# Attention of batches three to eight in quarters of TensorE's array, before a Strassen feed-forward

## The chip, the cores and the metric

The kernel runs on one core of a Trainium2 chip. The metric is the device time of one execution in microseconds, the median of several runs. The profile shows one execution: TensorE (PE, with its weight loads PEld), VectorE (DVE), ScalarE (ACT), GpSimd (POOL), SyncE (SP, which issues the DMAs) and the DMA engines.

## What is computed

Eight batches of eight heads, 576 positions, head width 64, all in float32 at both ends. Heads 0 to 3 look back over a plain window of 32 positions, heads 4 to 7 over 32 positions with a step of 4. The result goes through a feed-forward layer of width 2048.

```python
scores = scale * np.matmul(q, k.transpose(0, 1, 3, 2))
rel = pos[:, None] - pos[None, :]
mask_plain = (rel >= 0) & (rel < window)
mask_dil = (rel >= 0) & (rel < window * dilation) & (rel % dilation == 0)
...
attn = attn / (np.sum(attn, axis=-1, keepdims=True) + 1e-09)
return np.matmul(attn, v).astype(np.float32)
...
h = x @ w_in
g = np.maximum(0.01 * h, h)
return (g @ w_out).astype(np.float32)
```

## The kernel before

All matmuls are in float16. The tokens of two batches (1152) are three chunks of 384. For each chunk the first layer (`up`, L1057, and `up_pair`, L1091; the last three chunks by Strassen's seven products in `ups7`, L1191) writes `gt` through a Prelu on ScalarE, and the second layer goes by tiles of 128 tokens, the first four plainly (`down`, L1271), all others in groups of four with seven products for eight (`group`, L1361).

Attention feeds `xt`, the input of the first layer. The program treats the heads of a batch in four pairs (`vi`, called visits, in the order 2, 3, 0, 1; 2 and 3 are dilated), each in two units (`unit`, L815 on). A pair lies on 128 partitions, 64 for each head. A stationary block of keys holds 64 keys of both heads, column by column in turn, with zeros in the half that belongs to the other head, so that one 128 x 128 block gives the scores of both. A unit has three groups of matmuls on TensorE, each between other work: the scores (L899, five matmuls of up to 96 columns), the sums of the exponentials (L924, against a constant block) and the values (L918, five matmuls). Between them ScalarE takes the exponential (L907), VectorE multiplies it with the mask (L911) and, for plain pairs, adds what overlaps (L932); after them ScalarE takes the logarithm of the sums and the exponential of its negative (L943, L945) and VectorE multiplies the values with it into `xt` (L956). Scores and values take the three PSUM banks `sps`, `ops0` and `ops1` in turn.

For the first two batches (`EARLY`) queries and keys are loaded in long rows and turned by TensorE (`turn_in`, L743), and the mask comes as a matmul of a bias. For batches three to eight they are loaded in rows of 32 numbers, cast by GpSimd (L505), turned by VectorE in blocks of 32 (L708, L713, L720), and spread into the zero-padded blocks by copies on ScalarE, GpSimd and VectorE (L516, L517, L714). The values are cast twice for each pair, once for each head, into columns in turn (L505).

The order is planned by the program itself: each piece of work is a task with an estimated duration and the pieces that it needs, a list scheduler runs over them several times, and the tables `NUDGE` (shifts of priority by task number) and `HAND` (a fixed engine for a task) change its choice. `WHEN` gives the time at which a batch's attention is due. The result is a fixed order on each engine's queue; each engine then works strictly in that order.

Of the kernel before, what the change touches and what calls it, by code (L numbers as in the profile page):

```python
# [14 lines left out]
WIN = 32  # L15
# [3 lines left out]
WHEN = (3.92, 2.82, 39.64, 80.18, 115.4, 117.81, 161.72, 152.03)  # L19
PASSES = 8  # L20
SEVEN = (9, 10, 11)
SECOND = 'st01t'
ADDED = (2, 9)
LAPS = ("DVE", "POOL")
# [91 lines left out]
    "DVE", 1623: "POOL", 1629: "POOL", 1633: "ACT", 1728: "DVE", 1740: "DVE"}  # L116


HELD = 4


def _constants():
# [246 lines left out]
def kernel(  # L369
# [19 lines left out]
    NJ = DFF // 128  # L389
    SCALE = float(1.0 / np.sqrt(D))  # L390
    HS = S * D
    EARLY = 2
    VISITS = (2, 3, 0, 1)

    const_d = nc.inline_tensor(_constants(), name="consts").ap()
# [1090 lines left out]
    for b in range(EARLY):  # L1486
        take_slots(b)
# [180 lines left out]
```

## Time and profile before

| | |
|---|---|
| time, three runs | 294.31 to 294.81 us, median 294.36 us |
| span of the profiled execution (no other time is given for it) | 292.5 us |
| granted TensorE clock | 1.00 |
| VectorE, ScalarE, GpSimd busy | 78%, 75%, 41% of the span |
| DMA queue q1, share of the DMA engines' time | 65.0% |
| first and last scores of batches three to eight | 64.0 us, 231.8 us |

The page gives busy time by engine, the span in 40 slices, the chain of work that ended last, and the costliest groups of instructions with their mean duration. A duration of a matmul reaches from its start until its last result is written; the next matmul starts long before that. Where the distance from one to the next is needed, it is read from the starts in the timeline.

### The profile page before, as it was taken

The page shows a single profiled execution, that of the slowest core. Times are in us where ns is not written, and L with a number is a line of the kernel's source. Part 1 is how long each engine was busy: PE and PEld are TensorE (multiplying, and loading weights), DVE is VectorE, ACT ScalarE, POOL GpSimd, SP SyncE. Part 2 cuts the span into 40 slices and gives each one's busy share as a digit, 9 for nine tenths or more (in the row PEclk, how much of TensorE's full clock was granted, in tenths as well). Part 3 has the DMA queues.
Part 4 walks back from the last instruction along what each step waited for, and adds up shares of the span by engine and source line. Part 5 has one row for each costly group of instructions (what it writes and reads, how often), then busy time and mean ns, then how long its engine had stood idle before and what let it go on. Part 6 is the DMA issues. An engine that isn't in the chain of part 4 may idle for free.

```text
span 292.5 us, 7626 instructions
## 1 busy us (share of the span) xinstructions
PE 285.2 (97%) x2924; PEld 226.4 (77%) x2924; DVE 226.8 (78%) x437; ACT 218.9 (75%) x483; POOL 121.2 (41%) x173
## 2 busy tenths in 40 slices
PE   6899999999999999999999999999999999999995
PEld 2567776776787788677777877887688999999985
DVE  7877588674799789858839889897878889678672
ACT  3997987589869966878888987888767966755522
POOL 5420452458537746964873774653425000000000
PEclk9999999999999999999999999999999999999999
DMA  7999999799898959999799798751101210121133
GB/s 244 267 389 396 395 377 224 150 168 218 142 188 185 179 144 174 191 168 208 197 170 160 180 205 151 195 134 59 36 2 36 75 38 0 38 74 36 38 109 110
DMA packets 156068, 47.15 MB, mean 161 GB/s; under 512 B 136832, under 2 KB 153344, under 8 KB 156032
## 3 DMA queue, kind: packets, MB, share of 16 engines
q1 hardware_dynamic: 155344, 46.04, 65.0%
q10 hardware_dynamic: 688, 0.63, 0.6%
q8 instruction: 23, 0.38, 0.5%
q14 instruction: 13, 0.11, 0.1%
HBM read 37.22 MB, written 9.44 MB: 160 GB/s over the span
## 4 chain that ended last, share of the span: by engine, by line
PE 93%; ACT 2%; DVE 2%; DMA 1%; issue 1%; ACTq 0%; DVEq 0%
PE hps L1057 27%; PE fps L1361 23%; PE tp L1361 9%; PE hps L1191 5%; PE fps L1271 4%; PE hps L1091 4%; PE ops L1191 3%; PE ops L918 3%; PE ops L899 2%; PE sps L899 2%; PE ops L924 2%; PE sps L1191 1%; DMA con<-consts 1%; PE sps L924 1%; PE ops L1361 1%; PE sps L918 1%
## 5 line engine op out<-in xcount | busy, mean ns | idle before, releaser
L1057 PE MATMUL hps<-xt,w_in 128*128 128x384 f16 x488 | 94.7, 325 | 0.0
L1361 PEld LDWEIGHTS <-gt 128*128 128x128 f16 x768 | 73.0, 98 | 9.8 <-DVE gt L1347 0.2
L1073 ACT ACTIVATE gt<-hps 128x384 f16<-128x384 f32 x122 | 59.1, 487 | 13.7 <-PE hps L1057 12.7
L1057 PEld LDWEIGHTS <-w_in 128*128 128x128 f16 x512 | 44.9, 98 | 21.3 <-issue 0.3
L505 POOL CAST slots<-vst 128x576 f16<-128x576 f32 x55 | 46.0, 861 | 22.7 <-DMA vst<-in_v_dram 5.6
L505 POOL CAST nat<-stg 128x576 f16<-128x576 f32 (+1 forms) x52 | 34.6, 687 | 48.6 <-DVE gt L1347 15.1
L1361 PE MATMUL fps<-w_out,gt 128*128 128x256 f16 x368 | 46.7, 272 | 0.0
L911 DVE TENSOR_TENSOR ee<-ee,con 128x384 f16<-128x384 f16 (+1 forms) x48 | 20.6, 430 | 15.3 <-ACT ee L907 14.9
L945 ACT ACTIVATE rc<-rc 128x288 f32<-128x288 f32 (+1 forms) x64 | 27.2, 436 | 1.1
L956 DVE TENSOR_TENSOR xt<-ops,rc 128x288 f16<-128x288 f32 (+2 forms) x44 | 19.3, 445 | 9.7 <-ACT rc L945 4.9
L516 ACT COPY slots<-turned 64x512 f16<-64x512 f16 (+1 forms) x30 | 23.8, 799 | 0.8 <-DVE turned L708 0.5
L1214 ACT ACTIVATE gt<-vst 128x384 f16<-128x384 f32 (+1 forms) x24 | 16.0, 684 | 8.0 <-DVE vst L1210 8.0
L899 PEld LDWEIGHTS <-slots 128*128 128x128 f16 x308 | 18.1, 98 | 4.7 <-DVE slots L517 0.4
L517 POOL COPY slots<-turned 64x576 f16<-64x576 f16 (+2 forms) x25 | 16.7, 675 | 11.2 <-ACT slots L516 3.5
L907 ACT ACTIVATE ee<-ops 128x416 f16<-128x416 f32 (+2 forms) x35 | 16.7, 487 | 3.6 <-PE ops L899 3.0
L918 PEld LDWEIGHTS <-slots 128*128 128x128 f16 x308 | 17.1, 97 | 2.8 <-ACT slots L504 0.6
L924 PEld LDWEIGHTS <-con 128*128 128x128 f16 x168 | 14.0, 97 | 5.9 <-issue 0.8
L708 DVE STREAM_TRANSPOSE turned<-nat 128x576 f16<-128x576 f16 x24 | 18.0, 759 | 0.1
L1390 ACT COPY stg<-fps 128x512 f32<-128x512 f32 (+1 forms) x20 | 10.4, 519 | 9.4 <-PE fps L1361 9.1
L907 ACT ACTIVATE ee<-sps 128x416 f16<-128x416 f32 (+2 forms) x29 | 14.4, 495 | 3.8 <-PE sps L899 2.7
L1347 DVE TENSOR_TENSOR gt<-gt 128x1024 f16<-128x1024 f16 x21 | 16.6, 789 | 0.3 <-PE fps L1361 0.2
L1191 PEld LDWEIGHTS <-w_in 128*128 128x128 f16 x192 | 16.2, 98 | 0.2
(158 smaller groups left out, 559.8 us busy)
## 6 DMA issues: line engine op xcount, KB each, us to landing
out_dram<-osb SPq DMA_DIRECT2D x32, 256.0 KB, 2.6
stg<-in_k_dram SPq DMA_DIRECT2D x48, 144.0 KB, 3.6
stg<-in_q_dram SPq DMA_DIRECT2D x48, 144.0 KB, 3.4
vst<-in_v_dram SPq DMA_DIRECT2D x16, 288.0 KB, 4.3
vst<-in_v_dram SPq DMA_DIRECT2D x32, 128.0 KB, 3.2
gt<-in_moe_w_in_dram SPq DMA_DIRECT2D x6, 512.0 KB, 6.8
stg<-in_q_dram SPq DMA_DIRECT2D x3, 512.0 KB, 6.9
stg<-in_k_dram SPq DMA_DIRECT2D x3, 512.0 KB, 9.1
```

Source lines behind the costliest of these rows:

```text
L505: return ENG[e].tensor_copy(out=dst, in_=src)
L516: return nc.scalar.copy(out=dst, in_=src)
L899: nc.tensor.matmul(p_bank[:, c:c + w], slot(tn, KB + 128 * s, 0, 128, [1, 128]), slot(tn, qx, 0, 128, *qd), start=first or not by_pe, stop ...
L907: lambda e: nc.scalar.activation(out=et[:, 0:n], in_=p_bank[:, 0:n], func=AF.Exp, scale=SCALE), prio)
L911: lambda e: nc.vector.tensor_tensor(out=et[:, 0:n], in0=et[:, 0:n], in1=con[:, table:table + n], op=ALU.mult), prio,
L918: nc.tensor.matmul(at(dst, 0, 128, o, *od), lhs(s), et[:, c:c + w], start=i == 0, stop=i == len(steps) - 1, skip_group_check=True)
L924: nc.tensor.matmul(at(p_bank, 0, 128, o, *od), block_ones, at(et, 0, 128, c, *cd), start=i == 0, stop=i == len(rows) - 1, skip_group_check ...
L945: lambda e: nc.scalar.activation(out=rt, in_=rt, func=AF.Exp, scale=-1.0), prio)
L1057: nc.tensor.matmul(ht[:, 0:n], at(w_in, 0, 128, vi * DFF + j // 2 * 256 + j % 2, [2, 128]), at(xt[m % 2], 0, 128, vi * 1152 + x0 + x, [1, n]),
L1073: lambda e: nc.scalar.activation(out=gt[c % NG][:, j * n_c + x:j * n_c + x + n], in_=ht[:, 0:n], func=AF.Prelu, alpha=0.01),
L1191: nc.tensor.matmul(bk[:, n * i:n * i + n], w(v, 2 * z + i), x(v), start=first and i == 0 and v == 0, stop=i == 1 and v == 1, skip_group_ch ...
L1361: nc.tensor.matmul(bk[:, x:x + HN], tl[:, off + j * step:off + j * step + 128], rhs(j), start=first and x == 0 and j == 0, stop=j == HJ - ...
```

## The change

Batches three to eight no longer go through `unit`. Their attention goes through `burst`: one task on TensorE that holds the sums and values of one pair and the scores of a later one. Each matmul is 64 x 64: it names a quarter of the array by `tile_position`, takes its rows from 64 partitions and writes 64 partitions. Four such matmuls stand together, one for each quarter, and the two row halves write to different PSUM banks. No block is padded with zeros.

- Heads of a pair are neighbours (0 and 1, 2 and 3, ...), no longer one apart. So the rows of `w_in` for a pair are 128 rows on end, and one DMA loads them at once.
- Batch three (`PACKED = 3`) loads in long rows and is turned by TensorE, as the first two are. From batch four on, queries and keys lie as two pairs side by side, and the scores of two visits must be there before the values of either.
- The sums and values of a pair come one burst after its scores in batch three and two bursts after in the others.
- One exponential, one mask multiplication, one logarithm and one reciprocal for a pair, over 576 to 896 columns in two PSUM banks, in place of two each over 288 to 416; the additions for overlaps are gone. The multiplication into `xt` has two parts.
- A burst takes four banks: `ops0`, `ops1`, `sps` and one that the group of the second layer does not use just then (`lent`).
- Queries and keys of plain pairs are turned by VectorE straight to their place; those of dilated pairs need one more copy each, on GpSimd or ScalarE (L910). The copies into padded blocks and the constant for them are gone. The values are cast once for a pair.
- Values are loaded in 14 DMAs a batch in place of 8.
- All PSUM is one tile `psum`, cut into the same eight banks. `NUDGE` and `HAND` have new numbers throughout, since the tasks are others; `WHEN` has only its first two entries, and bursts are placed every `PACE` groups of the first layer from `PLACE` on.

```diff
-WHEN = (3.92, 2.82, 39.64, 80.18, 115.4, 117.81, 161.72, 152.03)
+WHEN = (3.92, 2.82)
...
+PLACE = 20.0
+PACE = 4.7
+SWITCH = 0.3
...
-    EARLY = 2
+    EARLY, PACKED = 2, 3
...
+        if b >= EARLY:
+            lv = []
+            for i in range(2):
+                p = 64 * i
+                if g:
+                    lv += [load(queue, at(vs, p, p + 64, 128 * n, [320, 4], [1, 128]),
+                                dram(v, base + (256 * n + 2 * i) * D, [4 * D, 64], [HS, 4], [1, 128]),
+                                256, 512, v_old, prio + 0.01 * n) for n in range(2)]
...
-            src = dram(moe_w_in, heads_of(vi)[0] * D * DFF + x, [DFF, 64], [2 * D * DFF, 2], [1, 1024])
+            src = dram(moe_w_in, 128 * vi * DFF + x, [DFF, 128], [1, 1024])
...
+    def burst(now, then, prio, lent):
+
+        seats = [ops[0], ops[1], lent, sps]
+        room, mine = {}, {}
+        for bk in seats:
+            room[key(bk)], mine[key(bk)] = grab(bk)
...
+        def product(bk, x, od, lhs, rhs, p, q, first, last):
+            p0, p1, q0, q1 = quarter(p, q)
+            jobs.append(lambda: nc.tensor.matmul(
+                at(bk, q0, q1, x, *od), lhs(p0, p1, q), rhs(p0, p1), start=first, stop=last,
+                skip_group_check=True, tile_position=(p0, q0)))
...
+            for n, two in enumerate(list(zip(sums_of(vi, 0), sums_of(vi, 1)))
+                                    + list(zip(values_of(vi, 0), values_of(vi, 1)))):
...
+            for _, c, w, keys, asks in places(b2, v2):
+                for p in range(2):
+                    for q in range(2):
+                        def lhs(p0, p1, _, k=keys[q]):
+                            return slot(t2, KB + k[1], p0, p1, k[0])
...
+            t_l = add("ACT", 0.07 + S / 1200.0, [t_b] + r_old,
+                      lambda e: nc.scalar.activation(out=at(rt, 0, 128, 0, [288, 2], [1, 288]),
+                                                     in_=both(1, 224, None, [1, 288]), func=AF.Ln), prio)
+            t_r = add("ACT", 0.105 + S / 1200.0, [t_l],
+                      lambda e: nc.scalar.activation(out=rt, in_=rt, func=AF.Exp, scale=-1.0), prio)
...
+    pairs, due = [], []
+    for b, vi in [(b, vi) for b in range(EARLY, B) for vi in VISITS] + [(B, None)] * 2:
+        pairs.append((due.pop(0) if due else None, (b, vi) if b < B else None))
+        if b < PACKED:
+            due.append((b, vi))
+        elif b < B and vi % 2:
+            due += [(b, vi - 1), (b, vi)]
```

The first place is TensorE in the middle of the program. Before, the values of one dilated unit stand between two groups of the first layer (`hps` is their bank, `ee` the exponentials, `slots` the values of a pair). Rows that only repeat are left out.

```order
L1057 MATMUL hps_103<-xt_87,w_in 128x384
L918 LDWEIGHTS slots
L918 MATMUL ops_101<-ee_81,slots 128x96
L918 MATMUL ops_101<-ee_81,slots 128x80
L918 MATMUL ops_101<-ee_81,slots 128x2x16
L1057 LDWEIGHTS w_in
L1057 MATMUL hps_102<-xt_87,w_in 128x384
```

Now, again between groups of the first layer (L1378 is its line now), a burst stands in one piece: sums against the constant `con`, values from `slots`, and the scores of a later pair.

```order
L1378 MATMUL psum<-xt_78,w_in 128x384
L1256 LDWEIGHTS con
L1256 MATMUL psum<-ee,con 64x96
L1256 MATMUL psum<-ee,con 64x64
L1256 MATMUL psum<-ee,con 64x32
L1256 LDWEIGHTS slots
L1256 MATMUL psum<-ee,slots 64x64
L1256 MATMUL psum<-slots 64x96
```

What stood in three to six places of the queue stands in one, 64 to 68 matmuls long. There are 26 such pieces: the first and the sixth have scores alone, the last two none.

The second place is ScalarE. Before, the two units of a plain pair go through it one after the other, between the Prelu of the first layer (L1073).

```order
L907 ACTIVATE ee_81<-sps_104 128x416
L1073 ACTIVATE gt_88<-hps_103 128x384
L907 ACTIVATE ee_82<-ops_101 128x416
L1390 COPY osb_91<-fps_105 128x512
L943 ACTIVATE rc_83<-sps_104 128x288
L945 ACTIVATE rc_83<-rc_83 128x288
L943 ACTIVATE rc_84<-ops_101 128x288
L945 ACTIVATE rc_84<-rc_84 128x288
```

Now, at the fourth and the fifth burst: L1346 is the exponential of the scores, L1318 and L1321 the logarithm and the exponential of its negative, L1394 the Prelu.

```order
L1346 ACTIVATE ee<-psum 128x896
L1318 ACTIVATE rc<-psum 128x576
L1394 ACTIVATE gt_82<-psum 128x384
L1321 ACTIVATE rc<-rc 128x576
L1394 ACTIVATE gt_82<-psum 128x384 x3
L1346 ACTIVATE ee<-psum 128x2x384
L1394 ACTIVATE gt_82<-psum 128x384
L1318 ACTIVATE rc<-psum 128x576
```

Six instructions of a pair became three, each about twice as wide, and they stand closer together behind their burst.

More of the change, by code (lines that the diff above doesn't have):

```diff
@@ L119 @@
 HELD = 4
+TURN_AT = ('st01t', 'ssss0')
+DOWN_ON = (0, 1)
 def _constants():
@@ L696 @@
     x_done, x_used = {}, {b: [] for b in range(-2, B)}
+    seat_of = {'f': fps[0], 'g': fps[1], 's': sps, '0': ops[0], '1': ops[1], 't': tpb}
     def turn(b, vi, prio):
@@ L1176, in ups7 @@
             h = z // 2
-            ring5 = five if c > 9 else [hps[0], hps[1], ops[1]]
-            X, Y, Z = (ring5[(five_at[0] + i) % len(ring5)] for i in range(3))
+            X, Y, Z = (five[(five_at[0] + i) % len(five)] for i in range(3))
             five_at[0] += 3
@@ L1485 @@
     t_con = [None]
-    for b in range(EARLY):
+    for b in range(2):
         take_slots(b)
@@ L1516, in attend @@
         else:
-            banks = dict.fromkeys(VISITS, [sps, ops[0]] if b == 7 and 9 in SEVEN else three)
+            banks = dict.fromkeys(VISITS, three)
         for n, vi in enumerate(VISITS):
@@ L1525, with place, bursts @@
     wide_banks = {2: fps[0], 3: fps[1], 4: tp32, 5: sps, 6: ops[0], 7: ops[1]}
+    pairs, due = [], []
+    for b, vi in [(b, vi) for b in range(EARLY, B) for vi in VISITS] + [(B, None)] * 2:
+        pairs.append((due.pop(0) if due else None, (b, vi) if b < B else None))
+        if b < PACKED:
+            due.append((b, vi))
+        elif b < B and vi % 2:
+            due += [(b, vi - 1), (b, vi)]
+    assert not due
+    flow, lent, n_up, weights = [0], [tp32], [0.0], {}
+    def place(k):
+        return PLACE + PACE * k
+    def bursts(upto, prio):
+        while flow[0] < len(pairs) and place(flow[0]) <= upto:
+            now, then = pairs[flow[0]]
+            if then is not None:
+                b, vi = then
+                if vi == VISITS[0]:
+                    fetch(b, prio, 6.5)
+                if b < PACKED:
+                    if vi == VISITS[0]:
+                        turn_rest(b, prio)
+                    turn(b, vi, prio)
+                elif vi == VISITS[0]:
+                    for v in VISITS:
+                        turn(b, v, prio)
+                then = take(b, vi)
+            flow[0] += 1
+            burst(now, then, prio, lent[0])
     def ups(c, x, n, batches, js=(0, NJ)):
@@ L1592 @@
     order.sort(key=lambda t: (t.start, t.n))
-    slow = next(t for t in order if t.eng == "POOL" and t.kind == "cast" and t in ups_at[0].deps)
+    slow = next((t for t in order if t.eng == "POOL" and t.kind == "cast" and t in ups_at[0].deps), None)
     kept = [t for t in order if t.eng == "ACT" and t.start < ups_at[1].start]
-    if slow.start < kept[-1].start:
+    if slow is not None and slow.start < kept[-1].start:
         slow.eng, slow.start = "ACT", kept[-1].start + 1e-4
```

474 lines of the change are left out of this document (294 added, 180 removed), and 306 rows, old and new, of the table NUDGE.

## Prediction

> **What bounds the kernel now.** I read the page first (busy shares and the chain that ended last), then the busy time of each engine in two stretches, then the waits of TensorE, and last the timeline of TensorE around the attention of the later batches.
>
> ```profile
> PE 285.2 (97%) x2924; PEld 226.4 (77%) x2924; DVE 226.8 (78%) x437; ACT 218.9 (75%) x483; POOL 121.2 (41%) x173
> PE 93%; ACT 2%; DVE 2%; DMA 1%; issue 1%; ACTq 0%; DVEq 0%
> 24.00:236.00 212.00, 211.65 (x2166) 164.07 (x2163) 166.99 (x321) 172.13 (x386) 112.15 (x155) 1.00 0.76 172
> 236.00:292.50 56.50, 53.55 (x551) 49.85 (x549) 40.72 (x81) 29.15 (x58) 0.00 (x0) 1.00 0.17 57
> PE tp L743 <- ACT nat L504: 0.7, 1, 0.7
> PE ops L924 <- ACT ee L907: 0.3, 1, 0.3
> ```
>
> The first two lines are from the page, the next two are the stretches (span, then busy time of PE, PEld, DVE, ACT and POOL), the last two are waits. TensorE is busy for 211.65 of the 212 us from 24 to 236, at a granted clock of 1.00, and it is 93% of the chain. Its waits on another engine are single ones of 0.7 and 0.3 us. So the time of this kernel is the sum of TensorE's stream, and a change is worth what it takes from that stream, less the waits that it brings. A busy matmul overlaps the next one, so durations can't be added: what counts is the distance from the start of one group to the start of the next.
>
> ```profile
> 81.64 0.35 PE L899 MATMUL sps<-slots 128*128 128x96 f16 x5
> 81.83 1.03 PE L1361 MATMUL fps<-w_out,gt 128*128 128x256 f16 x8
> ...
> 101.69 0.34 PE L918 MATMUL ops<-ee,slots 128*128 128x96 f16 x5
> 101.88 0.33 PE L924 MATMUL ops<-ee,con 128*128 128x192 f16 x3
> 102.05 0.33 PE L918 MATMUL sps<-ee,slots 128*128 128x96 f16 x5
> ...
> 106.31 0.30 PE L924 MATMUL sps<-ee,con 128*128 128x32 f16 x3
> 106.45 0.35 PE L918 MATMUL ops<-ee,slots 128*128 128x96 f16 x5
> 106.64 1.03 PE L1361 MATMUL fps<-w_out,gt 128*128 128x256 f16 x8
> 107.52 0.29 PE L924 MATMUL ops<-ee,con 128*128 128x160 f16 x2
> 107.64 0.60 PE L1361 MATMUL fps<-w_out,gt 128*128 128x256 f16 x4
> ```
>
> Here the first column is the start. One group of scores (L899, five matmuls) holds TensorE for 81.83 - 81.64 = 0.19 us. A group of values (L918) holds it for 0.19 us (101.69 to 101.88, 106.45 to 106.64). A group of sums (L924) takes 0.17 us where it is dilated (three matmuls, 101.88 to 102.05), and 0.14 and 0.12 us for the two halves of a plain pair (106.31 to 106.45, 107.52 to 107.64).
>
> **What is removed.** Batches 3 to 8 have 24 head pairs of two units each.
>
> ```profile
> L899 PEld LDWEIGHTS <-slots x240: 95/98/99, 64.0 to 231.8; 128*128 128x128 f16 x120
> L918 PEld LDWEIGHTS <-slots x240: 95/98/99, 67.8 to 235.3; 128*128 128x128 f16 x120
> L924 PEld LDWEIGHTS <-con x132: 95/98/99, 66.3 to 234.8; 128*128 128x128 f16 x132
> ```
>
> These are the instructions of those batches alone, from 64 us on: 240 / 5 = 48 groups each of scores and values, and 132 matmuls of sums. Removed are 48 x 0.19 = 9.1 us of scores, 48 x 0.19 = 9.1 us of values, and 24 x 0.17 + 12 x 0.14 + 12 x 0.12 = 7.2 us of sums: 25.4 us together.
>
> **What is added on TensorE.** The scores of before stream 416 columns for a plain half in 0.19 us, so 0.46 ns a column. In the new bursts the 1584 matmuls of L1256 come in 396 sets of four, one for each quarter of the array. One quarter streams 448 + 416 + 416 = 1280 columns for a plain pair and 3 x 384 = 1152 for a dilated one, so 12 x 1280 + 12 x 1152 = 29184 in all. If the four quarters run side by side, that is 29184 x 0.46 ns = 13.4 us. Batch 3 is now turned by TensorE: 32 transposes and 4 for its last rows.
>
> ```profile
> 8.94 0.39 PE L791 MATMUL fps<-con,rest 128*128 128x128 f16 x4
> 9.16 0.39 PE L743 MATMUL fps<-con,nat 128*128 128x128 f16 x4
> ```
>
> Four transposes hold TensorE for 0.22 us, so 36 cost 2.0 us. The stream alone is 13.4 + 2.0 - 25.4 = **-10.0 us**.
>
> **Changing over.** TensorE enters and leaves the quarters 26 times. No matmul in quarters is in this trace, so I bound the price of one change-over.
>
> ```profile
> L899 PE MATMUL sps<-slots x110: 179/206/213, 64.2 to 231.8; 128*128 128x96 f16 x61, 128*128 128x80 f16 x22, 128*128 128x32 f16 x17, 128*128 128x64 f16 x10
> ```
>
> A matmul of 96 columns lasts 206 ns and streams for 96 x 0.46 = 44, so its last 0.16 us is a tail that the next matmul normally overlaps. Below: nothing, the quarters overlap with the full array just so. Above: the tail is waited out on entering and on leaving, 52 x 0.16 = 8.3 us. No row is nearer to one end than to the other, so I take one tail for each burst, 26 x 0.16 = 4.2 us, and keep both ends.
>
> The Trainium skill (TensorEngine Tiling (Array Packing), Key Properties) says that a change of the tiling mode, not of the tile alone, drains TensorE. It speaks for the upper end, no run so far shows it, and by it the sum would be 4.1 us higher than mine.
>
> **New waits.** Before, a unit's Exp, Ln and reciprocal are separate and short, and there are three PSUM banks in turn. A burst takes four banks at once (three of them always the same), and the next burst can't start before ScalarE and VectorE have emptied them.
>
> ```profile
> L907 ACT ACTIVATE ee<-sps 128x384 f16<-128x384 f32 x11 | 5.4, 489 | 0.7 <-issue 0.5 <-PE sps L899 0.2
> L907 ACT ACTIVATE ee<-sps 128x320 f16<-128x320 f32 x4 | 1.8, 438 | 0.3 <-PE sps L899 0.3
> L943 ACT ACTIVATE rc<-ops 128x288 f32<-128x288 f32 x27 | 10.8, 409 | 3.2 <-PE ops L924 3.1
> L945 ACT ACTIVATE rc<-rc 128x288 f32<-128x288 f32 x52 | 22.4, 442 | 0.9
> L956 DVE TENSOR_TENSOR xt<-ops,rc 128x288 f16<-128x288 f32 x38 | 16.8, 449 | 7.3 <-ACT rc L945 4.7 <-PE ops L918 1.3 <-PE ops L924 1.1
> L1073 ACT ACTIVATE gt<-hps 128x384 f16<-128x384 f32 x122 | 59.1, 487 | 13.7 <-PE hps L1057 12.7
> ```
>
> The two rows of L907 differ by 51 ns for 64 columns, 0.8 ns a column. So an Exp of 768 columns is some 489 + 384 x 0.8 = 0.80 us, Ln and reciprocal of 576 columns are 0.41 + 288 x 0.0008 = 0.64 and 0.44 + 0.23 = 0.67 us, and the products into xt (576 columns in two instructions, where 288 take 0.45 us) 0.9 us. With the tail of 0.16 the banks are free 3.2 us after a burst, if nothing stands between. In the order of ScalarE one or two Prelu of the first layer (487 ns) do stand between. Counted in the new order, the work between two bursts is mostly 3.7 to 6 us, but 2.6 us after the fourth (four groups of L1378, each four matmuls long), so there 3.2 + 0.5 - 2.6 = 1.1 us are bare; after the fifth and at four gaps of 3.7 us some 0.3 us each. I take 2.5 us in all; below none (a burst is itself longer by the change-over), above 6 us, if two Prelu more stand in the way at the five short gaps. Who is queued behind such a burst: all of TensorE, the up and down matmuls with it.
>
> **Off the path.**
>
> ```profile
> 150.00:200.00 50.00, 50.00 (x511) 39.33 (x510) 43.62 (x81) 42.52 (x95) 28.24 (x40) 1.00 0.82 170
> 200.00:236.00 36.00, 36.00 (x393) 30.20 (x392) 28.56 (x53) 27.99 (x66) 10.79 (x11) 1.00 0.09 31
> 122.74 6.92 SPq L489 DMA_DIRECT2D stg<-in_k_dram  x7
> 147.45 3.38 SPq L489 DMA_DIRECT2D stg<-in_q_dram  x4
> 134.85 0.61 SPq L489 DMA_DIRECT2D vst<-in_v_dram  x1
> ```
>
> ScalarE loses the 30 copies L516 and half its attention instructions, VectorE the additions for the overlaps and half of its mask instructions, GpSimd 24 casts of v and most of its copies: none is waited for, so they only give cover. The loads are nearer to the path. The next to last number of a stretch is the DMA share: 0.82 until 200 us, then 0.09, so the loads end near 200 us, while the last scores of before stand at 231.8. In the new order some 78 us of stream stand behind the last scores, which puts them near 208 us. SyncE issues v in 14 DMAs a batch where it issued 8, at about 0.6 us each (134.85), and the queries and keys of batch 3 in 6 where it took 16 of 0.9 us (7 in 6.92): 36 x 0.6 - 10 x 0.9 = 13 us more of its time, and outputs queue behind them. I cost that at nothing, covered by the 8 us that are left (and by batch 3's longer rows); if the cover fails, TensorE waits at the first burst of a late batch, up to 5 us in all. The columns of w_in in another row order are the same bytes and the first 24 us keep their plan: nothing, within 1 us.
>
> **Sum.** -10.0 + 4.2 + 2.5 = -3.3 us on a span of 292.5. The median of the runs, 294.36, lies 1.9 us over that span; that part stays. **Forecast 291.1 us.** Its own range is 287.5 to 293.7.
>
> **Rivals.**
> - *The change-over is free and the waits are covered.* For it: ScalarE and VectorE get lighter. Against: the four shared banks. -10.0 to -7: 284.4 to 287.5 us.
> - *The pipe runs empty at both ends of each burst (slower).* Place: the first matmul of L1256 after another line, and the first of another line after it. Price 8.3 us: 294.4 - 10.0 + 8.3 + 2.5 = 295.2 us, and up to 299 with 6 us of waits. It decides when a burst costs over (10.0 - 2.5) / 26 = 0.29 us beside its stream.
> - *The four quarters load weights too slowly.* A load is 98 ns for 128 columns (L899 PEld), half of it for 64. Four loads side by side then pace each set at 0.049 us in place of 13.4 / 396 = 0.034: 396 x 0.015 = 5.9 us more, 297.0 us. Against: before, loads are overlapped, since groups of five take 0.19 us and not 0.49. The Trainium skill (TensorEngine Tiling (Array Packing), Restrictions) says that column tiling switches the fast weight load off; if so, this is the case that it makes, and no row here can show it.
> - *The quarters don't run side by side: the change doesn't do what it says.* The shortest matmuls of before follow each other at 27 ns:
>
> ```profile
> 23.04 0.54 PE L1003 MATMUL ops<-ee,slots 128*128 128x16 f16 x14
> 23.42 0.32 PE L1057 MATMUL tp<-xt,w_in 128*128 128x384 f16 x1
> ```
>
> 14 in 0.38 us. 1584 x 0.027 = 42.8 us in place of 13.4: 320.5 us. Nothing in the trace excludes it but that the rows and columns of the quarters are disjoint.
> - *A batch lands late:* SyncE's 13 us more decide, once they exceed the 8 us of cover; for it, SyncE hardly pauses between 100 and 150 us. 13 - 8 = 5 us on top: 296.1 us.
> - *No change:* change-over at 5.8 us and waits at 4 or so eat the gain, 294.4 us.
>
> **How the numbers follow.** Forecast 0.48; free 0.13; no change 0.08; pipe empty 0.14; late batch 0.06; weight loads 0.04; no overlap 0.07. A measurement of this kernel can tell 0.2% (0.6 us) from no change. Faster 0.48 + 0.13 = 0.61, same 0.08, slower 0.14 + 0.06 + 0.04 + 0.07 = 0.31. The range reaches from the free case (284.4) to the empty pipe with the largest waits (299), and leaves out the last rival and the edges of two others, some 0.15.
>
> **What would show it.** In the timeline of the changed kernel, the distance from the first L1256 of a full burst to the next line is some 0.56 us of stream (13.4 / 24) plus the change-over: near 0.7 the forecast holds, near 0.9 the pipe runs empty, above 1.7 the quarters run in turn. In the waits of TensorE, L1256 on VectorE or ScalarE should sum to about 2.5 us, the largest after the fourth burst. TensorE stays over 95% of the span and over 90% of the chain. I am wrong if TensorE has idle time of several us elsewhere, on v or turned keys that land late, or if the first 24 us take longer.

## The result and the profile after

The changed kernel takes 326.9 us (median of four runs, 325.35 to 328.6) against 294.6 us before (294.31 to 294.82): 1.110 times as long, 95% interval 1.106 to 1.114. Forecast were 291.1 us. The profiled execution took 325.35 us, its span is 323.5 us. Further down, two of six runs of e1_banks and one of four of e2_split lay over 1.5% above the fastest of their kernel, and the medians given for these two are those of the other runs.

The first lines are from the page of the changed kernel: the span, the busy time of each engine, the chain that ended last, and four of the costliest groups (busy time, mean duration, then the idle time of the engine just before them and what ended most of it).

```profile
span 323.5 us, 9433 instructions
PE 290.9 (90%) x3932; PEld 219.3 (68%) x3932; DVE 213.3 (66%) x378; ACT 196.6 (61%) x398; POOL 90.9 (28%) x125
PE 69%; ACT 13%; DVE 6%; DMA 4%; SPq 4%; issue 2%; POOL 0%; DVEq 0%; POOLq 0%; ACTq 0%
L1378 PE MATMUL psum<-xt,w_in 128*128 128x384 f16 x512 | 99.2, 326 | 13.7 <-ACT ee L1346 5.8
L1335 DVE TENSOR_TENSOR xt<-psum,rc 128x448 f16<-128x448 f32 (+1 forms) x48 | 28.7, 630 | 24.2 <-PE psum L1378 10.9
L1346 ACT ACTIVATE ee<-psum 128x768 f16<-128x768 f32 (+1 forms) x24 | 20.7, 863 | 18.4 <-PE psum L1378 13.7
```

TensorE fell from 97% of the span to 90%, and from 93% of the chain to 69%; ScalarE and VectorE now hold 19% of it. What they wait for is odd. L1346 is the exponential of scores that a burst (L1256) has written, and L1335 multiplies the values of a burst; L1378 is a group of the first layer and writes other banks. Yet both wait longest for L1378, and L1378 waits for L1346. The waits of TensorE and of ScalarE in the same trace (time in total, times, longest):

```profile
PE psum L1378 <- ACT ee L1346: 5.8, 6, 1.6
PE psum L1378 <- DVE xt L1335: 4.4, 8, 0.6
PE psum L1681 <- ACT ee L1346: 3.7, 4, 1.0
PE psum L1681 <- DVE xt L1335: 1.7, 3, 0.6
PE psum L1256 <- DVE xt L1335: 1.2, 4, 0.4
```

```profile
ACT ee L1346 <- PE psum L1378: 13.7, 12, 2.7
ACT gt L1394 <- DVE xt L1335: 10.5, 9, 1.8
```

Half of the 24 exponentials of the bursts wait for a group that they don't read. One burst in the timeline (start, duration) shows how that goes:

```profile
188.29 0.37 PE L1256 MATMUL psum<-ee,con 64*64 64x96 f16 x20
188.50 0.39 PE L1256 MATMUL psum<-ee,slots 64*64 64x32 f16 x28
188.73 0.37 PE L1256 MATMUL psum<-slots 64*64 64x64 f16 x20
189.03 0.82 PE L1378 MATMUL psum<-xt,w_in 128*128 128x384 f16 x4
189.54 0.10 PEld L1681 LDWEIGHTS <-gt 128*128 128x128 f16 x1
189.90 0.92 ACT L1346 ACTIVATE ee<-psum 128x896 f16<-128x896 f32 x1 [1.01 <-PE psum L1378]
190.87 0.93 PE L1681 MATMUL psum<-w_out,gt 128*128 128x256 f16 x7 [1.00 <-ACT ee L1346]
```

The burst runs from 188.29 to 189.03, 0.74 us, as forecast. Its scores are done by 189.1 us, but the exponential starts only at 189.90, when the four matmuls of L1378 behind the burst have ended. It takes 0.92 us, and TensorE, whose next weights were loaded by 189.64, stands until 190.87. The group L1681 that waits writes neither bank that the exponential reads.

**Theory A.** All PSUM is now one tile, cut into banks in the order `tp32, ops0, ops1, sps, hps0, hps1, fps0, fps1`. An Exp, a Ln or a product reads two banks in one access, with the distance of the banks as its step: the Exp and the first product `ops0` and the lent bank, the Ln and the second product `ops1` and `sps`, which are neighbours here. If such an access is ordered against everything from its first to its last element, the Exp over `ops0` and `fps1` is tied to `ops1`, `sps`, `hps0`, `hps1` and `fps0` too: it waits for the results written there, and the next to write there waits for it. The planner knows nothing of that.

**Rivals.** B: the waits are true; four shared banks and a chain of Exp, Ln, reciprocal and two products are too slow for the bursts. C: late loads, or the new order. D: it matters to the chip, not to the waits, where banks lie.

### The profile page after: what moved, and what is told of

Its sections match the earlier page's. It is cut to its first block, busy times and chain, and to the rows that moved or that the text cites. A ratio compares the mean times of both kernels' runs of the same rounds, so it can differ in the third digit from the quotient of the medians.

```text
span 323.5 us, 9433 instructions
## 1 busy us (share of the span) xinstructions
PE 290.9 (90%) x3932; PEld 219.3 (68%) x3932; DVE 213.3 (66%) x378; ACT 196.6 (61%) x398; POOL 90.9 (28%) x125
## 4 chain that ended last, share of the span: by engine, by line
PE 69%; ACT 13%; DVE 6%; DMA 4%; SPq 4%; issue 2%; POOL 0%; DVEq 0%; POOLq 0%; ACTq 0%
PE psum L1681 27%; PE psum L1378 22%; PE psum L1511 9%; ACT ee L1346 5%; PE psum L1256 4%; SPq L655 4%; DMA stg<-in_k_dram 4%; DVE xt L1335 3%; ACT gt L1394 3%; PE psum L1412 2%; ACT slots L682 1%; ACT rc L1321 1%; ACT rc L1318 1%; PE psum L1591 1%; PE psum L924 1%
## 5 line engine op out<-in xcount | busy, mean ns | idle before, releaser
L1378 PE MATMUL psum<-xt,w_in 128*128 128x384 f16 x512 | 99.2, 326 | 13.7 <-ACT ee L1346 5.8
L1681 PEld LDWEIGHTS <-gt 128*128 128x128 f16 x768 | 74.5, 98 | 18.4 <-issue 6.4
L1394 ACT ACTIVATE gt<-psum 128x384 f16<-128x384 f32 x128 | 61.2, 491 | 37.5 <-PE psum L1378 24.7
L1378 PEld LDWEIGHTS <-w_in 128*128 128x128 f16 x512 | 47.8, 98 | 44.4 <-issue 20.2
L1681 PE MATMUL psum<-w_out,gt 128*128 128x256 f16 x512 | 63.1, 272 | 4.5 <-ACT ee L1346 2.8
L1335 DVE TENSOR_TENSOR xt<-psum,rc 128x448 f16<-128x448 f32 (+1 forms) x48 | 28.7, 630 | 24.2 <-PE psum L1378 10.9
L671 POOL CAST slots<-vst 128x640 f16<-128x640 f32 (+1 forms) x34 | 26.3, 794 | 37.4 <-DMA vst<-in_v_dram 14.3
L1346 ACT ACTIVATE ee<-psum 128x768 f16<-128x768 f32 (+1 forms) x24 | 20.7, 863 | 18.4 <-PE psum L1378 13.7
L1355 DVE TENSOR_TENSOR ee<-ee,con 128x768 f16<-128x768 f16 (+1 forms) x24 | 16.1, 669 | 22.2 <-ACT ee L1346 22.1
L1530 DVE TENSOR_TENSOR vst<-psum,vst 128x384 f32<-128x384 f32 x36 | 19.5, 553 | 6.5 <-PE psum L1511 3.5
L1318 ACT ACTIVATE rc<-psum 128x576 f32<-128x576 f32 x24 | 15.6, 649 | 3.7 <-PE psum L1256 3.2
L1681 PE MATMUL psum<-wst,gt 128*128 128x256 f16 x128 | 16.3, 273 | 0.6 <-DVE xt L1335 0.6
L682 ACT COPY slots<-psum 64x128 f16<-64x128 f16 (+3 forms) x25 | 11.5, 483 | 8.3 <-PE psum L982 6.9
L1321 ACT ACTIVATE rc<-rc 128x576 f32<-128x576 f32 x24 | 16.5, 685 | 0.1
```

Source lines behind the costliest of these rows:

```text
L671: return ENG[e].tensor_copy(out=dst, in_=src)
L1318: lambda e: nc.scalar.activation(out=at(rt, 0, 128, 0, [288, 2], [1, 288]), in_=both(1, 224, None, [1, 288]), func=AF.Ln), prio)
L1321: lambda e: nc.scalar.activation(out=rt, in_=rt, func=AF.Exp, scale=-1.0), prio)
L1335: lambda e, args=args: nc.vector.tensor_tensor(out=args[0], in0=args[1], in1=args[2], op=ALU.mult), prio))
L1346: lambda e: nc.scalar.activation(out=at(et, 0, 128, 0, [448, 2], [1, n]), in_=bass.AP(tensor=seats[0].tensor, offset=seats[0].offset, ap=[ ...
L1355: lambda e: nc.vector.tensor_tensor(out=at(et, 0, 128, 0, [448, 2], [1, n]), in0=at(et, 0, 128, 0, [448, 2], [1, n]), in1=at(con, 0, 128, ...
```

## Experiments

| kernel | median, us | times before, 95% interval |
|---|---|---|
| changed | 326.9 | 1.110 (1.106 to 1.114) |
| e1_banks | 311.4 | 1.058 (1.052 to 1.064) |
| e2_split | 312.5 | 1.056 (1.051 to 1.061) |
| e3_apart | 354.7 | 1.204 (1.201 to 1.207) |
| e4_half_issues | 301.6 | 1.023 (1.018 to 1.027) |
| e5_long_packets | 301.0 | 1.023 (1.017 to 1.028) |
| e6_act_issues | 325.5 | 1.103 (1.095 to 1.110) |
| e7_before_half | 294.5 | 1.000 (0.998 to 1.002) |
| e8_long_half | 299.7 | 1.017 (1.013 to 1.021) |
| e9_switch_mid | 304.0 | 1.033 (1.030 to 1.035) |
| e10_switch_first | 301.0 | 1.023 (1.020 to 1.025) |
| e11_after_long | 325.5 | 1.104 (1.100 to 1.108) |
| e12_last_spans | 300.5 | 1.019 (1.015 to 1.023) |
| e13_start | 300.2 | 1.018 (1.014 to 1.022) |
| e14_v_long | 299.7 | 1.016 (1.012 to 1.020) |
| e15_no_recip | 299.3 | 1.017 (1.013 to 1.021) |
| e16_long_half_again | 300.4 | 1.019 (1.015 to 1.022) |

### Where the banks lie: e1, e2, e3

**e1_banks** gives the same names other places. Every engine has the same instructions in the same order.

```diff
-    tp32, *ops, sps, hps0, hps1, fps0, fps1 = (psum[:, 512 * i:512 * i + 512] for i in range(8))
+    tp32, fps0, ops0, fps1, ops1, sps, hps0, hps1 = (psum[:, 512 * i:512 * i + 512] for i in range(8))
...
```

> Only the places of the eight banks inside the one PSUM tile change: fps0, ops0, fps1 become neighbours, ops1 and sps too, and hps0, hps1 go to the end, so that no access to two banks has an hps bank between them. Every engine's instructions and their order stay as they are in the changed kernel. Theory A (waits on banks that lie between the two that an Exp, a Ln or a product reads, which hold up results of L1378 and are waited for by them): the waits of TensorE at L1378 on ee (5.8 us) and on xt (4.4 us) and the Exp's wait on L1378 (13.7 us) go, the share of TensorE on the chain of waits returns above 85%, and the time falls from 326.9 to 284 to 302. Rival B (the waits are true: four shared banks and a chain of Exp, Ln, reciprocal and products that is too long for the pace of the bursts): 323 to 330. Rival C (late loads, casts and turned keys, or the new order): 323 to 330.

Measured: 311.4 us (309.25 to 313.26). The same burst, with the same work behind it, in its timeline:

```profile
178.63 0.37 PE L1256 MATMUL psum<-ee,con 64*64 64x96 f16 x20
178.84 0.39 PE L1256 MATMUL psum<-ee,slots 64*64 64x32 f16 x28
179.07 0.38 PE L1256 MATMUL psum<-slots 64*64 64x64 f16 x20
179.38 0.82 PE L1378 MATMUL psum<-xt,w_in 128*128 128x384 f16 x4
179.50 0.92 ACT L1346 ACTIVATE ee<-psum 128x896 f16<-128x896 f32 x1 [0.27 <-PE psum L1256]
180.04 1.91 PE L1681 MATMUL psum<-w_out,gt 128*128 128x256 f16 x16
```

The exponential starts 0.87 us after the burst began (in the changed kernel 1.61 us), is released by the burst itself, and L1681 follows L1378 with no wait at all. In the page of this kernel the chain reads:

```profile
PE 55%; SPq 12%; DMA 11%; DVE 10%; issue 5%; ACT 4%; POOL 2%; POOLq 0%; ACTq 0%; DVEq 0%
L1378 PE MATMUL psum<-xt,w_in 128*128 128x384 f16 x512 | 98.5, 328 | 1.1 <-ACT gt L1394 0.6
L1346 ACT ACTIVATE ee<-psum 128x768 f16<-128x768 f32 (+1 forms) x24 | 20.7, 862 | 8.3 <-PE psum L1256 6.9
```

The idle time ahead of L1378 fell from 13.7 to 1.1 us. But the time fell by 15.5 us only, short of the 25 us or more expected, and TensorE holds 55% of the chain where over 85% were expected: what took the place of these waits is SyncE's queue and the DMAs, 23% of the chain where they held 8%. B falls for this part, and a form of C stands behind it.

**e2_split** leaves the banks where they were and takes each Exp, Ln and product apart, one instruction for each bank.

```diff
-                  lambda e: nc.scalar.activation(out=at(et, 0, 128, 0, [448, 2], [1, n]),
-                                                 in_=bass.AP(tensor=seats[0].tensor, offset=seats[0].offset,
...
+                  lambda e: [nc.scalar.activation(out=at(et, 0, 128, 448 * h, [1, n]),
+                                                  in_=at(seats[2 * h], 0, 128, 0, [1, n]),
+                                                  func=AF.Exp, scale=SCALE) for h in range(2)], prio)
```

> The banks stay where the changed kernel has them; each Exp, Ln and product over two banks becomes two instructions of one bank each, 24 more Exp, 24 more Ln, 48 more products. Theory A: no access spans a foreign bank any more, so most of the loss goes as with the moved banks; the added instructions cost some 0.2 us each on ScalarE (66% busy) and some 0.1 us on VectorE, half hidden: 286 to 308. Rival D (it is where the banks lie that matters to the chip and not the waits): stays at 322 to 333. Rivals B and C: longer chains on ScalarE and VectorE, 326 to 336.

Measured: 312.5 us, as e1, although 96 instructions more run on ScalarE and VectorE. (ScalarE was 61% busy in the changed kernel; the 66% of the expectation are VectorE's.) So D falls: with the banks untouched, an access to one bank at a time does the same. Nor are ScalarE and VectorE what holds this kernel.

**e3_apart** puts `hps0` and `hps1` between `ops1` and `sps`, and changes nothing else.

```diff
+    tp32, ops0, ops1, hps0, hps1, sps, fps0, fps1 = (psum[:, 512 * i:512 * i + 512] for i in range(8))
```

> The changed kernel with hps0 and hps1 put between ops1 and sps, so that Ln and the second product span them too, beside Exp and first product in the batches that lend fps0 or fps1; instructions and order unchanged. Theory A: more waits of the same kind, TensorE also waits for rc at L1378, time 330 to 350. Rivals B, C and D: within 1% of 326.9.

Measured: 354.7 us, somewhat more than the 350 at the end of the range. The waits of TensorE:

```profile
PE psum L1378 <- DVE xt L1335: 17.8, 19, 1.7
PE psum L1378 <- ACT rc L1318: 7.8, 10, 1.1
```

Now Ln (L1318) and the second product span the two banks of the first layer, and L1378 waits for them, 29 times in all where it was 8 times on xt. Three kernels with the same instructions in the same order on every engine take 311, 327 and 355 us by the place of the banks alone. Theory A is shown.

### What stood behind it: e4 to e8 and e11

The busy time of each engine in two stretches (span, then PE, PEld, DVE, ACT and POOL, granted clock, DMA share, GB/s) of the kernel before, the changed one and e1:

```profile
24.00:100.00 76.00, 75.65 (x771) 55.98 (x768) 56.83 (x113) 62.51 (x140) 38.57 (x56) 1.00 0.97 237
100.00:200.00 100.00, 100.00 (x1006) 77.89 (x1004) 81.60 (x157) 81.63 (x183) 62.78 (x90) 1.00 0.85 174
```

```profile
24.00:100.00 76.00, 72.20 (x1006) 49.93 (x1002) 47.03 (x93) 56.01 (x125) 27.67 (x40) 1.00 0.95 241
100.00:200.00 100.00, 86.13 (x1402) 60.95 (x1401) 63.08 (x106) 60.22 (x110) 36.09 (x53) 1.00 0.80 155
```

```profile
24.00:100.00 76.00, 72.31 (x996) 50.22 (x995) 47.56 (x93) 56.85 (x127) 28.09 (x39) 1.00 0.96 240
100.00:200.00 100.00, 91.67 (x1458) 67.41 (x1457) 68.97 (x119) 62.72 (x116) 38.33 (x56) 0.98 0.85 168
```

From 100 to 200 us TensorE is idle for 13.9 us in the changed kernel and still for 8.3 us in e1, with the DMA engines at 0.85. Theory S: SyncE issues too much. Theory P: the 16 engines move the small packets no faster.

**e4_half_issues** is e1 with half as many issues for queries, keys and a part of the values, in the same packets; **e5_long_packets** is e1 with as many issues, in long packets; **e6_act_issues** is e1 with the values of heads 0 to 3 issued by ScalarE; **e7_before_half** is the kernel before with half the issues of queries and keys.

The load of queries and keys in e4, and then in e5:

```diff
-                lo = [load("SP", at(st, 32 * a, 32 * a + 32, 0, [32, 36], [1, 32]),
-                           dram(src, base + (a // 2) * 2 * HS + (a % 2) * 32,
-                                [D, 32], [32 * D, 36], [1, 32]),
...
+                lo = [load("SP", at(st, 32 * a, 32 * a + 64, 0, [32, 36], [1, 32]) if a % 2 == 0 else None,
+                           dram(src, base + (a // 2) * 2 * HS, [32, 64], [32 * D, 36], [1, 32]),
...
```

```diff
+                lo = [load("SP", at(st, 32 * a, 32 * a + 32, 0, [1, 1152]),
+                           dram(src, base + a * HS, [1152, 32], [1, 1152]),
...
```

> The kernel with the moved banks (e1_banks), but the q and k loads of batches three to eight in two issues of 64 partitions in place of four of 32, and the values of heads 0 to 3 in four issues of 128 partitions in place of eight of 64: the same bytes in the same packets of 128 and 256 B, 64 issues of SyncE fewer; the data land in other rows, so attention works on rows in another order. Theory S (the issues of SyncE bound the loads: 259 against 229 before, 17.6 to 20.6 us of issuing in each 20 us from 60 to 180 us): 64 issues by 0.75 us are 48 us of SyncE less, loads arrive in time, waits of TensorE behind late data (some 18 us between 60 and 200 us) go: 290 to 299. Theory P (the 16 engines move the small packets no faster): 306 to 316, as e1_banks. Rival B (waits between TensorE, ScalarE and VectorE over the four shared banks): 306 to 316.

> The kernel with the moved banks, but each q and k load of batches three to eight reads 32 rows of 4608 contiguous bytes instead of 36 pieces of 128 B for each of 32 partitions: as many issues and as many bytes, but 92,160 packets of 128 B (74 us of the 16 engines) become some 2,560 long ones (about 30 us by the 4096 B packets of the same trace); the data are other pieces of q and k. Theory P: 290 to 299. Theory S, if an issue costs what it costs: 305 to 316; if the long issues (1 to 2 us) are SyncE held back by full queues, part of it comes too: 297 to 306. Rival B: 306 to 316.

> The kernel with the moved banks, but the 48 loads of the values of heads 0 to 3 of batches two to seven are issued by ScalarE's queue at the place the plan gives them, not by SyncE's; all is computed. Theory S: SyncE has 36 us of issues fewer, ScalarE 24 us more (0.5 us each by the three that it issues at the start) beside its 64%, and stands in line where a buffer is not free yet: 292 to 304. Theory P and rival B: 308 to 325.

> The kernel before with the q and k loads of batches three to eight in two issues of 64 partitions in place of four of 32 (48 issues fewer, same bytes and packets, rows in another order). Its TensorE waits for nothing for 97% of the time, and its issues are on time by the kernel's own plan. All theories: 291 to 296, within 1% of before; if faster than 291, late loads had held the kernel before too.

Measured: 301.6, 301.0, 325.5 and 294.5 us. Either edit alone (e4, e5) takes 10 us from e1; the kernel before gains nothing. The waits behind late data that the edits could take away were less than the some 18 us of the expectation: TensorE is idle for 11.5 us in e1 from 60 to 200 us. Issues of keys in SyncE's timeline, in e1 (first) and e5 (second):

```profile
110.25 3.33 SPq L655 DMA_DIRECT2D stg<-in_k_dram  x3
184.77 0.46 SPq L655 DMA_DIRECT2D stg<-in_k_dram  x1
188.01 1.72 SPq L655 DMA_DIRECT2D stg<-in_k_dram  x1
```

```profile
107.89 1.53 SPq L655 DMA_DIRECT2D stg<-in_k_dram  x3
```

and the time that the packets of queue q1 took, as a share of the 16 engines' span, again e1 and e5:

```profile
q1 hardware_dynamic: 146608, 46.60, 63.0%
```

```profile
q1 hardware_dynamic: 57008, 46.60, 54.1%
```

Three loads of keys hold SyncE for 3.33 us in short packets and 1.53 us in long ones, and in e1 itself one such load holds it for 0.46 us at 184.77 and for 1.72 us at 188.01. So an issue has no fixed price, and Theory S fails in its sum: e4 has 64 issues fewer, but by its timeline SyncE issues for 88.3 us of the stretch from 100 to 200 us, where it is 90.8 us in e1 (71.3 us in e5). That an issue lasts until the engines have taken what stands before it fits these numbers. It is not shown: a price that also grows with an issue's own packets isn't excluded, and why e4 gains as much as e5 with a SyncE that issues as long stays open. Shown is that easing either end is enough. TensorE is then busy again from 100 us on; e5:

```profile
24.00:100.00 76.00, 71.41 (x985) 48.87 (x982) 46.67 (x93) 55.56 (x125) 29.27 (x41) 1.00 0.87 252
100.00:200.00 100.00, 99.20 (x1585) 73.06 (x1583) 75.62 (x126) 68.79 (x128) 42.81 (x60) 1.00 0.64 170
```

e6 missed what S expected by over 20 us and lies at the upper end of what P and B expected. Its page names the DMAs themselves, and among them the values that ScalarE now issues:

```profile
PE psum L1681 26%; PE psum L1378 16%; DMA vst<-in_v_dram 14%; PE psum L1511 9%; PE psum L1256 4%; DMA stg<-in_q_dram 3%; SPq L655 3%; PE psum L1412 2%; ACT ee L1346 2%; PE psum L924 2%; DVE slots L683 1%; DMA stg<-in_k_dram 1%; POOL nat L67
```

Waiting for SyncE became waiting for the landing. The Trainium skill (DMA: Bandwidth & Descriptors, Issuing engines are not separate DMA queues) says that issuing from several engines saves only the sequencer's time, since all feed the same engines; in this run nothing was gained, 325.5 against 311.4 us. Why 14 us were lost was not taken apart; the granted clock of e6, 0.97, was lower than that of any other kernel here.

**e8_long_half** has both edits, **e11_after_long** puts the long packets into the changed kernel with its own banks.

> The moved banks with long packets and with the halved issues together (q and k loads of batches three to eight read 4608 contiguous bytes a partition in two issues of 64 partitions, values of heads 0 to 3 in four issues). If issues and packets were two separate bounds, each still standing when the other was eased, the time falls from 301 by most of what was left to the 291.1 of the prediction: 291 to 296. If both eased the same queue (an issue takes as long as the 16 engines need to drain what stands before it) and what is left of the loss lies in the first 80 us, where the loads of the weights and of batches one to three are unchanged: 299 to 302.

> The changed kernel with its own places of the banks and the long packets: the false waits stay, the loads are eased. If the two losses stand side by side (each counts whatever the other does): 326.9 less the 12 us that the same edit took from e1_banks, 313 to 317. If late loads hide behind the false waits: 321 to 327. If the false waits are only felt because loads are late: 301 to 306.

Measured: 299.7 and 325.5 us. e8 gains at most 2 us over e4 and e5, as the second case expected. That speaks for one queue but doesn't prove it, since in e5 TensorE already had only 0.8 us of idle time left from 100 to 200 us. And e11 is 1.4 us faster than the changed kernel only, so in that kernel the late loads are hidden: the false waits hold TensorE back by more than the loads do. Four medians give the two prices, that of the loads to within some 2 us, since the runs of e1 lie that far apart. With eased loads the false waits cost 325.5 - 301.0 = 24.5 us; without false waits the loads cost 311.4 - 301.0 = 10.4 us; the two together cost 326.9 - 301.0 = 25.9 us and not their sum.

### The price of a change-over: e9, e10

One small matmul of the whole array goes into 22 bursts, in e9 between values and scores (22 more pairs of changes), in e10 at their start. The line of e9, where `n_now` is the number of the first matmul of scores (e10 has 0 in its place):

```diff
-            for job in jobs:
+            for n, job in enumerate(jobs):
+                if now and then and n == n_now:
+                    nc.tensor.matmul(seats[0][:, 0:16], ident, con[:, 0:16], start=True, stop=True, skip_group_check=True)
```

> The kernel with moved banks and long packets (e5_long_packets), with one more matmul of the whole array, 16 columns, in each of 22 bursts, between its sums and values and its scores: 22 more changes from quarters to the whole array and back. Against e10_switch_first, which has the same 22 matmuls at the start of the bursts, where TensorE is on the whole array anyway. A free change-over: equal within 1 us. The price of the prediction, one 0.16 us tail for each pair of changes: e9 is 3.5 us longer. Both bounds of it: 0 to 7.0 us.

> The control for e9_switch_mid: the same 22 small matmuls of the whole array at the start of the bursts. 22 by some 0.05 to 0.1 us above e5_long_packets: 301 to 304.

Measured: 304.0 and 301.0 us (intervals 1.030 to 1.035 and 1.020 to 1.025): 3.0 us for 22 pairs, 0.14 us a pair, where the forecast took 0.16. The Trainium skill (TensorEngine Tiling (Array Packing), Key Properties) says that a change of the tiling mode drains TensorE; a price is there, about half of the 0.32 us that two full tails would be.

### What is left above the forecast: e12 to e16

Both losses eased, the kernel stands some 9 us above 291.1. **e12_last_spans** takes apart the last accesses that span a foreign bank, **e13_start** moves the transposes of the leftover rows, **e14_v_long** loads values in long packets too, **e15_no_recip** leaves the bursts' reciprocals out, all on e8; **e16_long_half_again** is e8.

The edits of e13 and of e15:

```diff
+    at_n = {t.n: t for t in order if t.kind != "w"}
+    for n, x in ((23, 4.66), (22, 5.75), (149, 6.36), (152, 7.05), (154, 7.06), (155, 7.07), (151, 7.08)):
+        at_n[n].start = x
```

```diff
-                      lambda e: nc.scalar.activation(out=rt, in_=rt, func=AF.Exp, scale=-1.0), prio)
+                      lambda e: None, prio)
```

> e8_long_half with the last accesses that span a foreign bank taken apart: while lent is tp32 (the first bursts), the Exp and the first product go over one bank at a time, so that fps0 and fps1 no longer lie between tp32 and ops0. Theory A: the waits of TensorE in the groups on ee (1.4 us in two places, the longest 0.9 near 70 us) go, 297.9 to 299.2 against 299.7; no more, since the rest of the 8.6 us above 291.1 lies in the first 24 us, in the loads up to 80 us that were left as they are, and in TensorE waiting at the up matmuls for a result that ScalarE takes up after an Exp, a Ln and a reciprocal (about 2 us from 83 to 92 us). If foreign banks were behind most of what is left: 292 to 296.

> e8_long_half with the transposes of the leftover rows (L982), their two casts and their four copies placed behind the first turned queries in the order of batch one; nothing else moves. If the start is what holds it: TensorE no longer waits 1.3 to 2.4 us at L982, 1.5 to 3 us less than e8 of the same call. If those rows are needed as early by the scores that follow, the wait turns up there: within 0.7 us of it.

> e8_long_half, with the values of heads 0 to 3 of all batches in contiguous pieces too (1280 or 2304 B in place of 256 B, other data): some 14 us of the 16 engines fewer, 3 us of it before 60 us. If loads still hold it: 2 to 5 us less than e8 of the same call. If not: within 0.7 us.

> e8_long_half without the reciprocals of the bursts (24 Exp of 0.69 us left out, so values are multiplied by the logarithm of their sum): 16.5 us of ScalarE less, each behind a burst, where results of the up matmuls stand in line. If that chain holds TensorE: 1.5 to 4 us less than e8 of the same call. If not: within 0.7 us.

> e8_long_half again, as the measure for the other three of this call: 298.5 to 301.

Measured: 300.5, 300.2, 299.7, 299.3 and 300.4 us. All intervals overlap that of e16: none of the four is shown to hold the kernel, though 1 us or so by any of them can't be excluded. What I expected of e12 did not come. In e8 the groups of the second layer wait for ee twice, 1.4 us in all; in e12 (L1690 there) 0.4 us of this is left, and once they stand for 1.1 us that the trace puts down to no engine:

```profile
PE psum L1690 <- issue: 1.1, 1, 1.1
```

What they stand for there is not shown. What can be said is where the rest of the 9 us lies. The stretches of e8, and then the first 24 us of the kernel before and of e8:

```profile
24.00:100.00 76.00, 72.87 (x1001) 50.64 (x999) 49.37 (x97) 57.54 (x127) 28.47 (x41) 1.00 0.92 254
100.00:200.00 100.00, 99.19 (x1635) 73.10 (x1636) 74.77 (x124) 67.45 (x125) 45.09 (x61) 1.00 0.72 169
```

```profile
0.00:24.00 24.00, 19.96 (x214) 12.43 (x215) 19.09 (x37) 17.57 (x40) 9.04 (x18) 1.00 0.94 308
```

```profile
0.00:24.00 24.00, 19.54 (x193) 12.71 (x194) 16.83 (x31) 15.61 (x38) 10.96 (x21) 0.93 0.89 281
```

From 24 to 100 us TensorE is idle 2.8 us longer than before (75.65 - 72.87), and in the first 24 us it is busy 0.4 us less, at a clock of 0.93. That clock shows no effect: of the five runs of e16, the one with a granted clock of 1.00 took 300.7 us, the four with 0.993 or 0.994 took 299.6 to 301.1 us. The cause of this idle time is not settled. But most of the 9 us isn't idle time. The busy times of e8, from its page:

```profile
PE 285.7 (96%) x3932; PEld 219.1 (74%) x3932; DVE 210.0 (71%) x378; ACT 196.2 (66%) x398; POOL 91.0 (31%) x125
```

TensorE is busy for 285.7 us, where it was 285.2 before. The forecast's -10.0 and 4.2 would have left 279.4. So the change took nothing from TensorE's busy time even with both losses eased, and no kernel of the study beats the one before.

## Why the prediction was wrong

**The quarters and what is removed: right.** The four quarters run side by side: 20 matmuls of sums hold TensorE for 0.21 us (188.29 to 188.50), 0.01 us each, where they would take 0.027 in turn. A full burst takes 0.74 or 0.75 us, and "near 0.7 the forecast holds" was the mark. All 612 matmuls that went (L899, L918 and L924 from 64 us on) held TensorE for 25.7 us in the trace of before, taken from each start to the next, where the forecast had 25.4. The rival of the weight loads isn't borne out: it took a load of 49 ns as the pace, but a load takes 110 ns while a set of four sums goes by in 0.042 us (0.21 / 5).

**The change-over: right in kind and about right in size.** 0.14 us a pair by e9 and e10 against 0.16. In the timeline of e1 (first), and in its chain in order of time (second: start, duration), the way into a burst shows as well:

```profile
178.22 0.49 PE L1378 MATMUL psum<-xt,w_in 128*128 128x384 f16 x2
```

```profile
105.50 1.31 PE psum L1378 x8
```

Eight matmuls of L1378 hold 1.31 us, so two hold 0.33; the burst could start at 178.55 and starts at 178.63, 0.08 us late. With the 0.74 us inside, a full burst takes 0.82 us where 0.56 of stream and 0.16 were forecast: 0.10 us more, some 2.5 us over 26 bursts.

**The stream as a whole: some 6 us too good.** The forecast let TensorE's busy time fall by 5.8 us; in e8 it rose by 0.5. Of these 6.3 us the longer bursts are 2.5. The 36 transposes of batch three held TensorE for about 2.5 us instead of 2.0. The rest, some 3 us, lies in the other lines and was not taken apart; part of it can be short waits, since a matmul counts as busy until its last result is written.

**The new waits: the step that failed.** The prediction said: "the next burst can't start before ScalarE and VectorE have emptied them", and "I take 2.5 us in all", with 6 us as the upper end. It priced the true waits alone, of a burst on its own four banks. Those were small: L1256 waits for the products 1.2 us in the changed kernel and 0.2 us in e8. In e1, where loads are late, they were 4.0 us, above the 2.5 but within the 6. But the same edit that made one instruction read two banks made these instructions hold, and wait for, all banks that lie between. The waits came on L1378 and L1681, lines that the prediction saw only queued behind a burst, never waiting for its banks themselves, and they cost 24.5 us (e11 against e5) where the whole term was 2.5. The one tile `psum` and the two-bank accesses were part of the change as it was described, and what they tie together was priced at nothing. None of the rivals held this.

**Off the path at nothing: failed second, and hidden by the first.** "I cost that at nothing, covered by the 8 us that are left", up to 5 us if the cover fails. It fails, by 10.4 us (e1 against e5). The sum of 13 us of SyncE's time took issues at a fixed 0.6 or 0.9 us, but the same issue takes 0.46 or 1.72 us in e1, and long packets alone cure the loss with as many issues. The rival of the late batch named the right place, at 5 us in place of 10.

**The first 24 us within 1 us: not refuted.** The changed kernel in that stretch:

```profile
0.00:24.00 24.00, 18.57 (x173) 11.75 (x174) 16.50 (x31) 14.79 (x37) 11.03 (x21) 0.93 0.87 276
```

The granted clock fell from 1.00 to 0.93, and TensorE is busy 1.4 us less than before (19.96). But this differs from trace to trace: it is 19.29 in e7, which is as fast as the kernel before, and 18.2 to 19.8 in the traces of the new order. Moving the leftover rows alone (e13) brought nothing.

**The sum.** 291.1 + 9.9 (e5 above the forecast: mostly more busy time of TensorE, 2.5 of it longer bursts, the rest spread and open) + 24.5 (false waits) + 1.4 (loads on top of them, within the spread of the runs) = 326.9 us.

## To carry to other kernels

When one instruction is widened to read two buffers through a step, look at what lies between them: if the order is kept by ranges, everything in between is tied to that instruction. Here putting the two side by side cost no instruction. A cover of some microseconds on an engine that issues DMAs was worth little here, where the DMA engines behind it were busy for 85% of the time: don't add up its issues at a fixed price. After removing a wait, look at the chain again before adding up the gain: here the second loss was invisible until the first was gone.

## What the chip showed beside it

Weight loads of the quarters are not shorter than those of the whole array. The instructions of L1256 in e1 (minimum, median and maximum duration in ns, first and last start):

```profile
L1256 PEld LDWEIGHTS <-slots x1104: 102/110/168, 65.1 to 234.9; 64*64 64x64 f16 x184
```

110 ns for 64 columns, against 98 ns for 128 before. The Trainium skill (TensorEngine Tiling (Array Packing), Restrictions) says that column tiling switches the fast weight load off, which this row fits; what else could make the loads longer wasn't tried. It costs nothing here: 20 sums with 20 loads (107 ns each) take 0.21 us, and even the five of one quarter, 0.53 us one after another, don't fit in that. So loads overlap with each other, within a quarter too, and with the matmuls.
